# Soft mixture of experts, first half: the down products of one token block as seven half-size products

## The chip, the cores and the metric

One core of a Trainium2 chip runs the whole program in one launch. TensorE (PE) multiplies a 128 x 128 weight tile with up to 512 columns and sums into PSUM, VectorE (DVE), ScalarE (ACT) and GpSimd (POOL) do the elementwise work, and SyncE (SP) issues the DMAs. The metric is the time of one execution on the device in microseconds, the median of several runs.

## What is computed

Three steps follow each other, all in float32 outside and inside: attention with a decay, a gated feed-forward network, and a soft mixture of 8 experts in which every token goes through every expert. The change lies in the last one. There are N = 2304 tokens (4 batches of 576), D = 512, F = 1024 hidden columns for each of E = 8 experts.

```python
def _moe2_ref(x, w_gate, w1, w2):
    P = np.exp(x @ w_gate - max)
    for _ in range(8):                       # balance rows and columns
        P /= P.sum(1, keepdims=True) + 1e-09
        P /= P.sum(0, keepdims=True) + 1e-09
        P *= N / E
    out = np.zeros((N, D))
    for e in range(E):
        h = np.maximum(x @ w1[e], 0.0)       # up product, relu
        ye = h @ w2[e]                       # down product
        out += P[:, e:e + 1] * ye
    return out
```

## The kernel before

**Precision.** Every operand of a product is kept as two tensors, a high part (a copy on ACT, which rounds) and a low part (value minus high part, mostly a subtraction on POOL through the helper `rest`, L163). A product of two such operands is three matmuls (`three`, L171, and the loops in `prod` and `mult`): high with high, high with low, low with high.

**Order of the work.** Attention and the gated network fill the time to about 681 us. Then come 64 slices i = (ph, e, s): two halves `ph` of the tokens (batches 0 and 1, then 2 and 3), in each half 8 experts, and for each expert 4 slices of 256 hidden columns. Slices 0 to 31 are the first half, 32 to 63 the second. A half has two token blocks g of 576 tokens.

**A unit.** For each slice and block `eup(i, g)` (L810) makes one unit. It computes the up product of the block as seven products of half size (`prod`, L827, seven times 6 matmuls of 288 columns into the tile `pa`). Sums of the inputs were made beforehand: those of `x` in `xload` and `xforms`, those of the weights in `wload`, on DVE (`sm` for the first matrix, L749, `sd` for the second, L767). The products are put together by copies `m`, `u` from PSUM (`keep`, L834, ACT), adds `c` (`comb`, L839, DVE) and a relu. Between the seven products a unit runs pieces of down product, handed in as `between` and taken by `fill`.

**Down products in the first half.** `relu` writes the high part `ah` (ACT) and the low part `al` (L849, DVE; from `c`, which lies in SBUF, as `al<-c`, or straight from PSUM as `al<-pa`). The two tiles of `hs[i]` hold all 1152 tokens, in two buffers each. `edown` (L1076) takes tiles of 128 tokens: 6 matmuls of 512 columns into `py` and one DVE add into `acc` (L1098). The second unit of slice i carries tiles 0 to 3 of slice i, the first unit of slice i + 1 carries tiles 4 to 8. A scheduler sets the order of the instructions here, on every engine.

**Down products in the second half.** The relu's result stays in one piece, `rr` (ACT, L844). `form(i, g)` (L890) makes from it the seven left operands: copies on ACT, sums `td` and low parts on POOL (L930 and L163). `fast` (L953) then makes 512 tokens by seven products of half size, in six pieces `s1` to `s6`, here called steps 1 to 6. Step 1 has 12 matmuls of 256 columns, the others 6 each, for two tiles m each, and behind each tile's matmuls stands an add into `acc` (`addto`, L951). Steps 1, 3, 5 and 6 write into the same two PSUM tiles `xy`: step 5 overwrites in place what the adds of step 3 read, step 6 what those of step 5 read. Steps 2 and 4 share the two tiles `zz`. The 64 tokens that are left of each block (`edges`, `eg`) are one tile of `slow`. `queued()` (L885) ties each group of matmuls behind the one before it, so PE's order is the order of the program.

**Weights.** `wload(i)` (L728) loads both matrices of a slice, makes sums, high and low parts, and `wsave(i - 1)` stores all of the slice before to DRAM for the second half, whose `wback` reads them back. The sums `sm`, `sd` (and `td`) share one buffer, so `sm` of one slice waits until the low part `sl` made from `sd` is done. From slice 8 on `xforms` makes and stores the second half's forms of `x` on the side.

**PSUM.** In the first half `ps_z` has 1 bank, `ps_y` (for `py`) 2 and `ps_a` (for `pa`) 5; in the second half `py` and `pa` have 4 each.

## Time and profile before

| | us |
|---|---|
| median of 3 runs | 2187.18 |
| the runs | 2181.81, 2187.18, 2188.16 |
| the profiled execution | 2184.39 |
| its span, first to last instruction | 2182.6 |
| PE busy in the span | 2146.4 (98%) |
| slices 5 to 30, each | 23.54 |
| slices 35 to 62, each | 22.58 |

The time of an execution is the span and 1.8 us around it. Durations in the rows are of the profiled execution. A matmul's own duration in a row is longer than its share of PE, since matmuls overlap: what one costs is read from the starts of those that follow each other. The granted clock of PE is 1.00 of full speed in both halves of the experts.

### The profile page before, as it was taken

The numbers are of one execution on the slowest core, as the hardware profiler recorded it, in microseconds if no ns is written. First come the engines' busy times: TensorE is split into PE (matmuls) and PEld (weight loads), VectorE is DVE, ScalarE is ACT, GpSimd is POOL, SyncE is SP. The second block draws the span as 40 slices with busy tenths as digits, with TensorE's granted clock in tenths as the row PEclk, the third lists the DMA queues.
The fourth block names the chain that finished last, engine by engine and source line by source line (L and its number), as shares of the span: only waits on it lengthen the run. The fifth ranks groups of instructions, "written<-read, shape, count | busy, mean of one in ns | idle before, by whom it ended". The sixth has DMA issues, their size and how long they took to land.

```text
span 2182.6 us, 39368 instructions
## 1 busy us (share of the span) xinstructions
PE 2146.4 (98%) x14941; PEld 1990.3 (91%) x14941; DVE 1382.9 (63%) x2981; ACT 976.5 (45%) x2405; POOL 1121.5 (51%) x1125
## 2 busy tenths in 40 slices
...
GB/s 224 281 234 209 228 173 195 207 159 127 282 175 109 279 191 217 277 202 241 228 238 224 239 225 191 227 377 126 193 170 164 198 146 207 156 178 186 154 209 82
DMA packets 151773, 443.58 MB, mean 203 GB/s; under 512 B 14996, under 2 KB 52224, under 8 KB 139936
## 3 DMA queue, kind: packets, MB, share of 16 engines
...
## 4 chain that ended last, share of the span: by engine, by line
PE 82%; DMA 5%; DVE 4%; ACT 3%; POOL 3%; issue 2%; SPq 0%; POOLq 0%; ACTq 0%; DVEq 0%
PE pa L827 30%; PE py L171 24%; PE py L969 14%; PE pm L171 10%; DMA st<-wf 2%; PE ps_o L444 1%; PE ps_t L416 1%; PE ps_s L320 1%; DMA lgd<-ls 1%; ACT np L295 1%; ACT lead L127 1%; DVE al L849 1%; DVE lead L128 1%; POOL w2l L163 1%; POOL w1l L163 1%
## 5 line engine op out<-in xcount | busy, mean ns | idle before, releaser
L827 PE MATMUL pa<-xf,w1h 128*128 128x288 f32 x3584 | 739.9, 295 | 3.6 <-ACT u L834 2.5
L827 PEld LDWEIGHTS pa<-xf,w1h 128*128 128x128 f32 x3584 | 581.7, 188 | 27.1 <-ACT u L834 3.4
L951 DVE SCALAR_TENSOR_TENSOR acc<-py,lg,acc 128x256 f32<-128x256 f32 (+1 forms) x759 | 386.7, 536 | 219.6 <-PE py L969 189.4
L827 PE MATMUL pa<-xf,w1l 128*128 128x288 f32 x1792 | 523.4, 295 | 0.0
L827 PEld LDWEIGHTS pa<-xf,w1l 128*128 128x128 f32 x1792 | 335.5, 188 | 4.5
L171 PE MATMUL pm<-xh,w 128*128 128x288 f32 x1536 | 327.2, 298 | 1.6 <-ACT xh L459 0.9
L171 PEld LDWEIGHTS pm<-xh,w 128*128 128x128 f32 x1536 | 251.7, 188 | 6.8 <-issue 2.7
L171 PE MATMUL py<-w2h,ah 128*128 128x512 f32 x608 | 239.6, 394 | 4.5 <-DVE acc L1098 4.4
L171 PE MATMUL py<-w2l,ah 128*128 128x512 f32 x608 | 239.2, 393 | 0.0
L171 PE MATMUL py<-w2h,al 128*128 128x512 f32 x608 | 238.5, 393 | 0.0
L1098 DVE SCALAR_TENSOR_TENSOR acc<-py,lg,acc 128x512 f32<-128x512 f32 x252 | 187.2, 746 | 77.9 <-PE py L171 76.6
L171 PE MATMUL pm<-xl,w 128*128 128x288 f32 x768 | 227.3, 296 | 0.7 <-POOL xl L163 0.7
L834 ACT COPY u<-pa 128x288 f32<-128x288 f32 x256 | 101.2, 396 | 212.2 <-PE pa L827 211.8
L163 POOL TENSOR_TENSOR al<-td,ah 128x1024 fp32r<-128x1024 f32 x60 | 144.6, 2410 | 74.6 <-ACT ah L944 74.6
L171 PE MATMUL py<-ah,w 128*128 128x288 f32 x768 | 175.2, 300 | 7.2 <-DVE th L544 3.8
L163 POOL TENSOR_TENSOR al<-th,ah 128x288 fp32r<-128x288 f32 x96 | 79.9, 833 | 194.4 <-ACT ah L545 187.0
L163 POOL TENSOR_TENSOR sl<-sd,sh 128x1024 fp32r<-128x1024 f32 (+1 forms) x40 | 79.6, 1998 | 193.6 <-ACT sh L770 193.5
L849 DVE SCALAR_TENSOR_TENSOR al<-c,ah 128x288 fp32r<-128x288 f32 x192 | 156.3, 829 | 26.5 <-ACT ah L848 23.8
L844 ACT ACTIVATE rr<-c 128x288 f32<-128x288 f32 x192 | 85.4, 445 | 183.5 <-DVE c L839 183.5
L171 PEld LDWEIGHTS pm<-xl,w 128*128 128x128 f32 x768 | 144.5, 188 | 3.0 <-issue 1.4
L839 DVE TENSOR_TENSOR c<-pa,u 128x288 f32<-128x288 f32 x256 | 115.0, 449 | 44.4 <-ACT u L834 32.4
L930 POOL TENSOR_TENSOR td<-rr 128x512 f32<-128x512 f32 x60 | 77.9, 1298 | 126.7 <-ACT eg L905 120.5
...
## 6 DMA issues: line engine op xcount, KB each, us to landing
...
```

What stands on the lines that cost most here:

```text
L127: nc.scalar.activation(out=g, in_=g, func=AF.Relu, scale=8.0, bias=base)
L163: return (eng or nc.gpsimd).tensor_tensor(out=out, in0=src, in1=hi.bitcast(F32), op=ALU.subtract)
L171: ins = nc.tensor.matmul(out=ps, lhsT=a, rhs=b, start=(i == 0), stop=(i == n - 1))
L827: last_pa[0] = nc.tensor.matmul(out=ps, lhsT=w[:, MW[m - 1], k], rhs=x[:, m - 1, hl, k], start=(first and n == 0), stop=(n == len(ops) - 1 ...
L834: nc.scalar.copy(out=t, in_=ps)
L839: last_u[0] = nc.vector.tensor_tensor(out=t, in0=in0, in1=in1, op=ALU.add)
L844: nc.scalar.activation(out=rr[i, g][:, PLACE[f, j]], in_=src, func=AF.Relu)
L849: nc.vector.scalar_tensor_tensor(out=al[:, f, tk], in0=src, scalar=0.0, in1=ah[:, f, tk].bitcast(F32), op0=ALU.max, op1=ALU.subtract)
L930: nc.gpsimd.tensor_tensor(out=t[:, 0:2], in0=b[:, 1:3], in1=b[:, 0:2], op=sub)
L951: nc.vector.scalar_tensor_tensor(out=a, in0=src, scalar=lg[:, TP + t, e:e + 1], in1=a, op0=ALU.mult, op1=ALU.add)
L969: last_pa[0] = nc.tensor.matmul(out=ps, lhsT=x, rhs=y, start=(first and k == 0), stop=(k == 2), skip_group_check=not first)
L1098: nc.vector.scalar_tensor_tensor(out=a, in0=py, scalar=lg[:, t, e:e + 1], in1=a, op0=ALU.mult, op1=ALU.add)
```

## The change

In the first half, block 0 of slices 4 to 30 no longer goes through `edown` but through `form(i, 0)` and `fast(i, 0)`, as the second half does it. Slices 0 to 3 and 31 (the set `direct`) keep the tiles of 512 columns.

- A new function `unit1(i, g)` says what a unit carries. The first unit of slice i carries five tiles of 512 columns of slice i - 1, in the order 5, 4, 6, 7, 8. The second unit of slice i carries steps 1 to 6 of `fast(i - 1, 0)` and, in four pieces, the forms of block 0 of slice i (`front`, `three_`, `middle`, `four`).
- The 64 border tokens of block 0 are put ahead of block 1: `hs[i]` is now 64 + 576 tokens wide, tiles 4 to 8, and has one buffer each instead of two. `rr` of block 0 and the forms `fh`, `fl` have one buffer as well.
- The low part of block 0 is made on POOL (`fl`, from `rr`) and no longer by the four `al` of that block on DVE; those of block 1 stay on DVE.
- `wload2` takes the second matrix out of `wload`: its load, its sums `sd`, its parts and its save come one slice later.
- From slice 4 on PE's order in the first half is tied by `queued()`, in `prod`, `mult` and `edown`.
- The PSUM pools of 4 and 4 banks start at slice 4 instead of 32.
- The gate values of the first half are grouped as those of the second (512 tokens of each block, then the border). Two attention masks move into a pool of their own, freed after the attention.

In numbers of matmuls: 3654 of 256 columns instead of 2520, 1368 `py` of 512 columns instead of 2016. The `al<-c` of DVE go from 192 to 96.

**Order on DVE.** The first list is DVE in the kernel before, around the sums `sm` for the first matrix of slice 17 (`w_12333` is the loaded matrix; `x2` are two in a row).

```order
L849 SCALAR_TENSOR_TENSOR al<-c,ah 128x288 x2
L1098 SCALAR_TENSOR_TENSOR acc<-py,lg,acc 128x512
L767 TENSOR_TENSOR sd<-w_12079 128x256 x2
L1098 SCALAR_TENSOR_TENSOR acc<-py,lg,acc 128x512
L767 TENSOR_TENSOR sd<-sd,w_12079 128x256
L767 TENSOR_TENSOR sd<-w_12079,sd 128x256
L1098 SCALAR_TENSOR_TENSOR acc<-py,lg,acc 128x512
L839 TENSOR_TENSOR c<-pa,u_12289 128x288
L1098 SCALAR_TENSOR_TENSOR acc<-py,lg,acc 128x512
L849 SCALAR_TENSOR_TENSOR al<-c,ah 128x288
L749 TENSOR_TENSOR sm<-w_12333 128x256 x2
L749 TENSOR_TENSOR sm<-sm,w_12333 128x256
```

The second is DVE in the changed kernel in the second unit of slice 15, from the adds of step 1 on.

```order
L1016 SCALAR_TENSOR_TENSOR acc<-py,lg,acc 128x256 x2
L756 TENSOR_TENSOR sm<-w_12810 128x256 x2
L868 TENSOR_TENSOR c<-pa,m_12671 128x288
L756 TENSOR_TENSOR sm<-sm,w_12810 128x256
L1016 SCALAR_TENSOR_TENSOR acc<-py,lg,acc 128x256 x2
L756 TENSOR_TENSOR sm<-w_12810,sm 128x256
L881 SCALAR_TENSOR_TENSOR al<-c,ah 128x288
L1016 SCALAR_TENSOR_TENSOR acc<-py,lg,acc 128x256 x5
L868 TENSOR_TENSOR c<-pa,u_12766 128x288
L1016 SCALAR_TENSOR_TENSOR acc<-py,lg,acc 128x256
L1016 SCALAR_TENSOR_TENSOR acc<-py,lg,acc 128x512
L881 SCALAR_TENSOR_TENSOR al<-c,ah 128x288
```

The sums `sm` stood at the end of a unit, behind the adds; now they stand among the adds of steps 1 and 2, with an `al` behind them, and all of it ahead of the adds of step 3.

**Order on POOL.** Before, the low parts of one slice's weights make up POOL's round, from the `sl` of one slice to that of the next:

```order
L163 TENSOR_TENSOR sl<-sd,sh 128x1024
L163 TENSOR_TENSOR w1l<-w_12333,w1h 128x2x128 x3
L163 TENSOR_TENSOR w1l<-sm,w1h 128x4x2x128
L163 TENSOR_TENSOR w2l<-w_12079,w2h 128x1024
L163 TENSOR_TENSOR sl<-sd,sh 128x1024
```

After, in slice 15 (here `al` of 32 columns are the border tokens' low parts, `rr<-rr` the sums of the forms):

```order
L165 TENSOR_TENSOR al<-rr,ah 128x32
L165 TENSOR_TENSOR sl<-sd,sh 128x1024
L165 TENSOR_TENSOR fl<-rr,fh 128x256
L165 TENSOR_TENSOR al<-rr,ah 128x32 x2
L165 TENSOR_TENSOR fl<-rr,fh 128x512
L165 TENSOR_TENSOR al<-rr,ah 128x32
L999 TENSOR_TENSOR rr<-rr 128x2x256
L1000 TENSOR_TENSOR rr<-rr 128x256
L1001 TENSOR_TENSOR rr<-rr 128x256
L165 TENSOR_TENSOR fl<-rr,fh 128x1024
L165 TENSOR_TENSOR w2l<-w_12812,w2h 128x1024
L165 TENSOR_TENSOR w1l<-w_12810,w1h 128x2x128 x3
```

Between `sl` and the weights' low parts there now stand the low parts and sums of block 0's forms.

The core of the diff:

```diff
@@ -730,6 +731,9 @@
             return
         ph, e, s = slices[i]
         if ph:
+            if i == len(slices) // NPH:
+                wload2(i - 1, True)
+                wload2(i - 1)
             wback(i)
             return
         hold = ExitStack()
@@ -738,9 +742,12 @@
         if i == 1:
             hold.enter_context(tc.issue_after(last_u[0].ins))
         nc.sync.dma_start(out=st, in_=w1[e][:, c0:c0 + FS].rearrange("(k p) f -> p k f", p=P))
-        st2 = wst.tile([P, FS // P, DM], F32, tag="w2", name="w2")
-        last_w[0] = nc.sync.dma_start(out=st2, in_=w2[e][c0:c0 + FS, :].rearrange("(c p) d -> p c d", p=P))
-        wsave(i - 1)
+        if i == 0:
+            wload2(0, True)
+        elif i > 1:
+            wload2(i - 1, True)
+        wsave(i - 1, 0)
+        wsave(i - 2, 1)
         sm = wst.tile([P, 4, 2, P], F32, tag="sm", name="sm", bufs=1)
...
             parts(lo[:, o], src, hi[:, o], 2 if i < EARLY and src is sm else 1)
+        raws[i, 0] = [t.rearrange("p f k c -> p k f c") for t in (hi, lo)]
+        wts[i] = [(hi, lo)]
+        if i != 1:
+            wload2(max(i - 1, 0))
+
+    st2s = {}
+
+    def wload2(i, get=False):
+        ph, e, s = slices[i]
+        c0 = s * FS
+        if get:
+            st2s[i] = wst.tile([P, FS // P, DM], F32, tag="w2", name="w2")
+            last_w[0] = nc.sync.dma_start(out=st2s[i], in_=w2[e][c0:c0 + FS, :].rearrange("(c p) d -> p c d", p=P))
+            return
+        st2 = st2s.pop(i)
+        sub, add = ALU.subtract, ALU.add
+        wsp = (wsp0, wsp1)[i % 2]
...
-        wts[i] = ((hi, lo), (hi2, lo2), (sh, sl))
-        raws[i] = [t.rearrange("p f k c -> p k f c") for t in (hi, lo)] + [hi2, lo2, sh, sl]
+        wts[i] += [(hi2, lo2), (sh, sl)]
+        raws[i, 1] = [hi2, lo2, sh, sl]
 
     wq, raws = {}, {}
 
-    def wsave(i):
+    def wsave(i, part):
         if i < 0:
             return
-        wq[i] = []
-        for n, t in enumerate(raws.pop(i)):
+        wq.setdefault(i, [])
+        for n, t in enumerate(raws.pop((i, part))):
             shape = [P] + [int(x) for x in t.shape[1:]]
-            wq[i].append(dram.tile(shape, F32, name=f"wq{i}_{n}"))
-            nc.sync.dma_start(out=wq[i][n], in_=t.bitcast(F32))
+            wq[i].append(dram.tile(shape, F32, name=f"wq{i}_{2 * part + n}"))
+            nc.sync.dma_start(out=wq[i][-1], in_=t.bitcast(F32))
 
...
@@ -813,8 +838,12 @@
         x = xf[ph * NB + g]
         if ph:
             rr[i, g] = xst.tile([P, 4, HB], F32, tag="x", name="rr", bufs=2)
-        elif g == 0:
-            hs[i] = [hp_.tile([P, 2, NB * S], F32R, tag=t, name=t) for t in ("ah", "al")]
+        elif g:
+            hs[i] = [hp_.tile([P, 2, 64 + S], F32R, tag=t, name=t, bufs=1) for t in ("ah", "al")]
+        elif i in direct:
+            hforms[i, 0] = [formed(t, 4, HB) for t in ("fh", "fl")]
+        else:
+            rr[i, 0] = hp_.tile([P, 4, HB], F32, tag="rr", name="rr", bufs=1)
...
-            with queued() if ph else ExitStack():
+            with queued() if i > EDGES[0] else ExitStack():
...
-            t = hp_.tile([P, HB], F32, tag=tag, name=tag)
+            t = hp_.tile([P, HB], F32, tag="u", name=tag, bufs=4)
...
         def relu(f, j, src):
-            if ph:
+            if (i, g) in rr:
                 nc.scalar.activation(out=rr[i, g][:, PLACE[f, j]], in_=src, func=AF.Relu)
                 return
-            ah, al = hs[i]
-            tk = slice(g * S + j * HB, g * S + (j + 1) * HB)
-            nc.scalar.activation(out=ah[:, f, tk], in_=src, func=AF.Relu)
+            if g:
+                tk = slice(64 + j * HB, 64 + (j + 1) * HB)
+                hi, lo = (t[:, f, tk] for t in hs[i])
+            else:
+                hi, lo = (t[:, PLACE[f, j]] for t in hforms[i, 0])
+            nc.scalar.activation(out=hi, in_=src, func=AF.Relu)
             nc.vector.scalar_tensor_tensor(
-                out=al[:, f, tk], in0=src, scalar=0.0, in1=ah[:, f, tk].bitcast(F32), op0=ALU.max, op1=ALU.subtract)
+                out=lo, in0=src, scalar=0.0, in1=hi.bitcast(F32), op0=ALU.max, op1=ALU.subtract)
 
...
+    last1 = len(slices) // NPH - 1
+    EDGES = (3, last1)
+    direct = {i for i in range(last1 + 1) if i <= EDGES[0] or i == last1}
+
+    def formed(tag, n, w):
+        t = hp_.tile([P, 7 * FS], F32R, tag=tag, name=tag)
+        return t[:, 0:n * w].rearrange("p (n c) -> p n c", n=n)
+
+    def border(i):
+        h, l = hforms[i, 0]
+
+        def ends(n):
+            to, src = hs[i][n][:, :, 0:64], (h, l)[n]
+            for f in range(2):
+                for j in range(2):
+                    o, a = to[:, f, j * 32:(j + 1) * 32], src[:, PLACE[f, j], FS:HB].bitcast(F32)
+                    if n:
+                        nc.gpsimd.tensor_copy(out=o, in_=a)
+                    else:
+                        nc.scalar.copy(out=o, in_=a)
+        return [lambda: ends(0), lambda: ends(1)]
...
+        early = i <= last1
+        if early:
+            edges[i] = [t[:, :, 0:64] for t in hs[i]]
+        elif g == 0:
...
+        def front():
+            nc.scalar.copy(out=h[:, 0], in_=b[:, 0])
+            nc.scalar.copy(out=h[:, 1:3], in_=b[:, 2:4])
+            side(ends_hi)
+
+        def middle():
+            nc.gpsimd.tensor_tensor(out=t[:, 0:2], in0=b[:, 1:3], in1=b[:, 0:2], op=sub)
+            nc.gpsimd.tensor_tensor(out=t[:, 2], in0=b[:, 2], in1=t[:, 0], op=sub)
+            nc.gpsimd.tensor_tensor(out=t[:, 3], in0=b[:, 3], in1=t[:, 2], op=sub)
+
...
-        return [one, two, three_, four]
+        return [front, three_, middle, four] if early else [one, two, three_, four]
 
     def addto(i, a, src, t):
-        e = slices[i][1]
-        nc.vector.scalar_tensor_tensor(out=a, in0=src, scalar=lg[:, TP + t, e:e + 1], in1=a, op0=ALU.mult, op1=ALU.add)
+        ph, e, _ = slices[i]
+        lt = lg[:, ph * TP + t, e:e + 1]
+        nc.vector.scalar_tensor_tensor(out=a, in0=src, scalar=lt, in1=a, op0=ALU.mult, op1=ALU.add)
 
     def fast(i, g):
...
+            if slices[i] == (0, 1, 0):
+                for t in range(4):
+                    nc.scalar.mul(out=acc[:, t], in_=acc[:, t], mul=lg[:, t, 0:1])
...
-            tiles = (range(split, split + 3), range(split + 3, TP))[g]
-            downs = [lambda t=t: edown(d, [t]) for t in tiles]
+            downs = [lambda t=t: edown(d, t) for t in ((5, 4, 6), (7, 8))[g]]
...
+    def unit1(i, g):
+        d = i - 1
+        if g == 0:
+            eup(i, 0, [lambda t=t: edown(d, t) for t in (5, 4, 6, 7, 8)] if i else [])
+            return
+        downs = fast(d, 0) if i and d not in direct else []
+        if i in direct:
+            later = lambda: border(i)
+            downs += [lambda t=t: edown(i, t) for t in range(4)]
+        else:
+            later = lambda: form(i, 0)
+        forms = []
+
+        def begin():
+            forms.extend(later())
+            forms.pop(0)()
+        steps = [begin] + [lambda: forms.pop(0)() if forms else None] * 3
+        downs += [None] * (len(steps) - len(downs))
+        steps += [None] * (len(downs) - len(steps))
+
+        def both(a, b):
+            for f in (a, b):
+                if f:
+                    f()
+        eup(i, 1, [lambda a=a, b=b: both(a, b) for a, b in zip(downs, steps)])
+
+    def edown(i, t):
         ph, e, s = slices[i]
         wb = wts[i][1]
-        ah, al = hs[i]
-        for tt in tiles:
-            t = ph * TP + tt
-            ts_ = slice(tt * P, (tt + 1) * P)
-            py = rooms[0].tile([P, DM], F32, tag="y", name="py")
-            three(py, [((ah[:, c, ts_], al[:, c, ts_]), (wb[0][:, c], wb[1][:, c])) for c in range(2)])
-            a = acc[:, tt, :]
-            if ph == 0 and e == 0:
-
-                if s == 0:
-                    nc.scalar.copy(out=a, in_=py)
-                else:
-                    nc.vector.tensor_tensor(out=a, in0=py, in1=a, op=ALU.add)
+        py = rooms[0].tile([P, DM], F32, tag="y", name="py")
+        if t < 4:
+            j, c = t // 2, slice(t % 2 * P, (t % 2 + 1) * P)
+            left = [[x[:, PLACE[f, j], c] for x in hforms[i, 0]] for f in range(2)]
+        else:
+            c = slice((t - 4) * P, (t - 3) * P)
+            left = [[x[:, f, c] for x in hs[i]] for f in range(2)]
+        with queued() if i > EDGES[0] else ExitStack():
+            ins = three(py, [(left[c], (wb[0][:, c], wb[1][:, c])) for c in range(2)])
+        if i > EDGES[0]:
+            last_pa[0] = ins
...
-        if i == len(slices) // NPH:
+        if i == EDGES[0] + 1:
...
-            tiles = range(split) if g else range(split, TP) if i else ()
-            eup(i, g, [lambda t=t: edown(i if g else i - 1, [t]) for t in tiles])
+            unit1(i, g)
```

## Rows read from the trace of the kernel before

**Rows 1.** The page, busy us, share of the span and instructions of each engine.

```profile
PE 2146.4 (98%) x14941; PEld 1990.3 (91%) x14941; DVE 1382.9 (63%) x2981; ACT 976.5 (45%) x2405; POOL 1121.5 (51%) x1125
```

**Rows 2.** Stages: window, length; busy PE, PEld, DVE, ACT, POOL; clock, DMA, GB/s.

```profile
812.00:1405.00 593.00, 586.04 (x3434) 526.36 (x3433) 446.61 (x784) 240.54 (x531) 265.39 (x181) 1.00 0.62 225
1490.00:2143.00 653.00, 653.00 (x5032) 645.80 (x5031) 425.50 (x898) 300.85 (x811) 458.94 (x581) 1.00 0.46 174
```

**Rows 3.** Timeline, ACT (start, duration): copy of slices 5, 31, 35, 63's first product.

```profile
792.79 0.38 ACT L834 COPY m<-pa 128x288 f32<-128x288 f32 x1
...
1404.96 0.40 ACT L834 COPY m<-pa 128x288 f32<-128x288 f32 x1 [1.05 <-PE pa L827]
...
1511.14 0.40 ACT L834 COPY m<-pa 128x288 f32<-128x288 f32 x1 [0.35 <-PE pa L827]
...
2143.47 0.40 ACT L834 COPY m<-pa 128x288 f32<-128x288 f32 x1 [0.35 <-PE pa L827]
```

**Rows 4.** Timeline of PE, both halves of the experts.

```profile
1036.23 0.39 PE L171 MATMUL py<-w2h,ah 128*128 128x512 f32 x1
...
1037.38 0.39 PE L171 MATMUL py<-w2h,al 128*128 128x512 f32 x1
...
1526.76 0.28 PE L969 MATMUL py<-sh,ah 128*128 128x256 f32 x1
...
1527.47 0.43 PE L827 MATMUL pa<-xf,w1h 128*128 128x288 f32 x2
...
1527.87 0.42 PE L827 MATMUL pa<-xf,w1h 128*128 128x288 f32 x2
```

**Rows 5.** Timelines of POOL and DVE around 1366 us.

```profile
1366.08 2.50 POOL L163 TENSOR_TENSOR w1l<-w,w1h 128x256 fp32r<-128x256 f32 x3
...
1366.15 1.82 DVE L749 TENSOR_TENSOR sm<-w 128x256 f32<-128x256 f32 x2 [1.39 <-POOL sl L163]
1367.90 0.96 DVE L749 TENSOR_TENSOR sm<-sm,w 128x256 f32<-128x256 f32 x1
```

**Rows 6.** Timelines of POOL, DVE and PE, 1033 to 1040 us.

```profile
1035.58 2.62 POOL L163 TENSOR_TENSOR w2l<-w,w2h 128x1024 fp32r<-128x1024 f32 x1
...
1033.35 5.17 DVE L849 SCALAR_TENSOR_TENSOR al<-c,ah 128x288 fp32r<-128x288 f32 x2
...
1038.44 0.74 DVE L1098 SCALAR_TENSOR_TENSOR acc<-py,lg,acc 128x512 f32<-128x512 f32 x1
...
1039.23 0.50 PE L171 MATMUL py<-w2h,ah 128*128 128x512 f32 x1 [0.92 <-DVE acc L1098]
```

**Rows 7.** DVE groups, 812 to 1405 us: busy us, mean ns, idle before, releaser.

```profile
L849 DVE SCALAR_TENSOR_TENSOR al<-c,ah 128x288 fp32r<-128x288 f32 x152 | 125.3, 841 | 23.0 <-ACT ah L848 20.7
...
L749 DVE TENSOR_TENSOR sm<-w 128x256 f32<-128x256 f32 x48 | 28.0, 618 | 9.1 <-POOL sl L163 8.3 <-DMA wq<-sh 0.8
...
L767 DVE TENSOR_TENSOR sd<-w 128x256 f32<-128x256 f32 x48 | 18.3, 420 | 26.5 <-DMA w<-w 26.4
```

**Rows 8.** Waits of PE, 812 to 1405 us: total us, times, longest.

```profile
PE py L171 <- DVE acc L1098: 4.2, 6, 1.5
```

**Rows 9.** Timeline of DVE in the second half.

```profile
1527.32 0.88 DVE L951 SCALAR_TENSOR_TENSOR acc<-py,lg,acc 128x256 f32<-128x256 f32 x2 [0.61 <-PE py L969]
1528.81 0.48 DVE L951 SCALAR_TENSOR_TENSOR acc<-py,lg,acc 128x256 f32<-128x256 f32 x1 [0.62 <-PE py L969]
```

**Rows 10.** POOL groups, 1490 to 2143 us: busy us, mean ns, idle before.

```profile
L163 POOL TENSOR_TENSOR al<-td,ah 128x1024 fp32r<-128x1024 f32 x58 | 139.8, 2411 | 72.0 <-ACT ah L944 72.0
...
L930 POOL TENSOR_TENSOR td<-rr 128x512 f32<-128x512 f32 x58 | 75.3, 1298 | 120.5 <-ACT eg L905 120.5
L163 POOL TENSOR_TENSOR al<-rr,ah 128x512 fp32r<-128x512 f32 x58 | 75.1, 1294 | 0.0
L163 POOL TENSOR_TENSOR eg<-rr,eg 128x32 fp32r<-128x32 f32 x232 | 56.3, 253 | 1.5 <-ACT eg L905 0.4
L163 POOL TENSOR_TENSOR al<-rr,ah 128x256 fp32r<-128x256 f32 x58 | 42.7, 736 | 0.0
```

82 lines of the change are left out of this document (48 added, 34 removed).

## The prediction

> **What bounds the kernel now.** I read the page first: TensorE (PE) is busy 98% of the span [rows 1], so only two things can move the time: fewer or shorter matmuls, and places where PE waits. The table by stage then shows the two halves of the experts side by side [rows 2]: the first (812 to 1405 us) and the second (1490 to 2143 us). In the second half both token blocks already use the seven half-size products, so it is the model for what the first half is to become; but its POOL is busy 70% and its VectorE (DVE) 65%, while the first half has POOL at 45% and DVE at 75%. From the copies of each slice's first product I take the slice lengths [rows 3]: slices 5 to 30 take (1404.96 - 792.79)/26 = 23.54 us each, slices 35 to 62 take (2143.47 - 1511.14)/28 = 22.58 us. The order of PE gives what a slice holds: 84 up products of 288 columns and 54 down products of 512 before; in the second half 84 of 288, 84 of 256 and 6 of 512.
>
> Starts that follow each other give the price of one [rows 4]: 512 columns (1037.38 - 1036.23)/5 = 0.230 us, 256 columns (1527.47 - 1526.76)/6 = 0.118 us, 288 columns (1527.87 - 1527.47)/3 = 0.133 us. The first half's 84 x 0.133 + 54 x 0.230 = 23.6 us is its whole slice: it runs dense today. Its waits for DVE are small, 4.2 us in 593 us [rows 8].
>
> **What the change removes.** In 27 slices (4 to 30) the four tiles of the first block take 42 products of 256 columns instead of 24 of 512: 24 x 0.230 - 42 x 0.118 = 0.56 us less. The second half's slice, taken whole, gives (22.58 - 84 x 0.133 - 6 x 0.230)/84 = 0.119 us for the 256-column one, and so 0.52 us. I take 0.53 us, 27 times: -14 us.
>
> Here the Trainium skill speaks against the change: TensorE: Matmul & The Clock Gate, section Back-to-back issue gap, gives for sustained pairs of weight load and matmul 81 ns at 128 columns and 131 ns at 512. Between them 256 columns would be 98 ns (an estimate from that page), and 42 x 98 ns against 24 x 131 ns a loss of 1.0 us a slice, +26 us. The rows say 118 and 230, nearly halved, so the measurement decides and this gets no chance.
>
> **What it adds.** (1) ScalarE (ACT) gets some 3 us of copies a slice; it was busy 41% of this stage [rows 2] and stays far from full. Nothing waits on it that did not before. (2) POOL gets the low parts and sums of one block. In the second half two blocks cost 458.94/653 x 22.58 = 15.9 us a slice, one 7.9; with the 265.39/593 x 23.54 = 10.5 it has now, 18.4 of 23 us, 79%. As a sum that fits. (3) DVE loses the four low parts of that block and gets ten adds of 256 and two of 512 columns for four of 512; by count about +1 us, 65 to 80% busy. (4) Second-matrix forms a slice later: their loads and saves on SP move with them; the products that use them move a slice later too, so the cover (a whole slice of PE work) stays. If it were gone, the first 512-column product of a slice would wait for the low part. 0. (5) Slices 0 to 4 and the change to the second half (31, 32): the four downs missing from slice 4 come back as slice 31's; the reload of the x forms keeps 16 us of PE work in front of it. 0, within 4 us either way.
>
> **The term that decides: who holds DVE.** Where a DVE instruction reads two SBUF tensors (`sm`, `sd`, `al<-c`) while POOL runs one of its own, it ends only 0.3 us after POOL's instruction has ended. It shows [rows 5] in three POOL pieces back to back from 1366.08 to 1368.58 with two `sm` beside them in 1.82 us and a third in 0.96 us, one per POOL piece, in turns; `sd`, which finds POOL idle, takes 0.42 [rows 7]. `al<-c` averages 841 ns for the same reason [rows 7]. Adds into `acc` (one input in PSUM) are not held: 0.48 us each, 0.40 apart, with POOL at 70% [rows 2, 9]. The whole chain is there in the kernel of today [rows 6]: an `al` held until 1038.5 by a POOL piece that ends at 1038.20, the add behind it done at 1039.18, PE idle 0.92 us until 1039.23. The Trainium skill has a rule for it (SBUF — State Buffer, section Who interferes with whom: a DVE instruction with two SBUF inputs contends with a GpSimd instruction that reads SBUF, and whichever issues first blocks the other). By it half of the held instructions would be those that came first and waited for nothing, and the sum below would halve, to rival (b); [rows 5] show each `sm` behind a piece of its own, so the measurement decides.
>
> Today this costs PE little, since the first half's order leaves the `sm` for moments when POOL is idle and its hidden values are double buffered. The new order has neither. In 15 of the 27 slices (8, 12, 14 to 17, 21, 23 to 30) DVE stands as in the order shown: two adds, `sm` twice, `c`, `sm`, two adds, `sm`, `al`, then the adds of steps 3, 4, 5. `sm` can't start before POOL's `sl` is done, and right behind that `sl` POOL runs 0.74, 0.25 twice, 1.29, 0.25, 1.30, 0.74, 0.74 = 5.56 us without a gap (durations of the same pieces [rows 10]; the two 256-column sums taken like the 736 ns row).
>
> Now the second unit, from the start of step 1 (a product of 6 x 0.133 = 0.80, a step of 6 x 0.118 = 0.71). PE: step 1 to 1.42, product to 2.22, step 2 to 2.93, product, step 3 to 4.44, product, step 4 to 5.95, product to 6.75, step 5 to 7.46, product to 8.26, step 6 to 8.97, product to 9.77. An add starts 0.20 after its matmuls' slot (1526.76 + 3 x 0.118 = 1527.12, add at 1527.32) [rows 4, 9]. DVE unhindered: adds at 0.91 and 1.62 to 2.02; `sm` twice (0.34 each, 420 ns less the 0.08 overlap of rows 9) 2.70; `c` (0.38, estimated as 288/256 of that) 3.08; `sm` 3.42; adds 4.22; `sm` 4.56; `al` 4.94; first add of step 3 at 4.94. Step 5 overwrites what that add reads; it needs its end (0.48) and 0.05 [rows 6], so a start by 6.22. Slack: 1.28 us. The five held instructions each find POOL in a piece; the mean rest of one is the sum of squares over twice the sum, 5.18/11.1 = 0.47 us, together 2.3 us. Bounds: nothing, if POOL lies elsewhere, and the five longest pieces, 4.8 us; I take 2.3, since [rows 5] show one piece per instruction.
>
> So step 5 starts 1.0 us late (7.77). DVE still owes the other add of step 3, two of step 4, then step 5's (8.84, 9.62 with a `c` between); step 6's second half waits until 10.15 and the unit ends at 11.31, not 9.77: 1.5 us. Behind it the next unit's first 512-column product needs the last `al<-pa`, which stands behind two 512-column adds and an `al` that POOL can hold: 0 to 0.6, I take 0.2. So 1.7 us in these 15 slices. The other 12 have the `sm` elsewhere (ahead of step 1, or behind step 3): 0.3 to 1.7, I take 1.0. Sum 15 x 1.7 + 12 x 1.0 = +37 us. Most of today's 4.2 us of waits goes: -4.
>
> **Sum.** -14 + 37 - 4 = +19 us. The profiled execution took 2184.4 us, span 2182.6 and 1.8 around it; the median is 2187.2. 2187 + 19 = **2206 us**, slices of 24.3 us.
>
> **Rivals.** (a) PE stays dense: POOL's pieces fall beside the adds, as PE in the second half never waits for them. For it: the second half, with POOL busier than DVE. Against: there DVE has no two-SBUF instruction at all. -14 - 4 + 4 (0.15 a slice) = 2173 us. (b) Half the waits: 0.65 us a slice, 18 us, cancels: 2187 us. The point between (a) and mine is the slack: up to 1.28 us of held time in a unit costs step 5 nothing. (c) Held at the long pieces, 2.8 us a slice on the mean: 76 - 18 = +58, 2245 us; for it, POOL's 1024-column piece (2.41 us) standing across the last `al`; against, that POOL's order puts it past step 5. (d) The change not doing what it says: its order on PE has 1134 more 256-column products and 648 fewer of 512, so no.
>
> **Chances.** Forecast 0.53 (2195 to 2222), (a) 0.22, (b) 0.14, (c) 0.11. The range goes from (a) with all of today's waits gone, 2187 - 14 - 4 = 2169, to 2234; it leaves out a fifth of (a) and most of (c), some 0.15. This kernel can be told from no change at about 0.3% (6.6 us). Faster: (a) and a little of (b), 0.25; same: 0.14; slower: 0.61.
>
> **What would show it.** Slices 5 to 30 some 24.3 us long (22.9 under (a)); PE waiting for DVE `acc`, at the half-size products, 25 to 45 us in that stage; `sm` above 0.75 us on the mean (0.62 now) and `sd` still 0.42; POOL 70 to 80% busy. I would be wrong if `sm` stayed at 0.6, if the chain had DMA (the later second matrix) in PE's waits, or if slices before 5 or around 31 moved by more than 4 us.

## The result, and the profile after

The changed kernel takes 2214.85 us (median of 4 runs, 2212.88 to 2217.94) against 2185.8 for the kernel before (4 runs): a ratio of 1.0136, 95% interval [1.0115, 1.0157]. It is 29 us slower. The forecast was 2206, the range 2169 to 2234. The profiled execution is one of 2217.94 us, with a span of 2216.2, 33.6 us more than the 2182.6 of before.

The page after, busy us and share of the span of each engine, then the stage that answers to the first of [rows 2], with its columns: window, length, busy PE, PEld, DVE, ACT, POOL, clock, DMA share, GB/s.

```profile
PE 2157.6 (97%) x15427; PEld 2016.9 (91%) x15427; DVE 1422.1 (64%) x3089; ACT 1041.5 (47%) x2614; POOL 1355.9 (61%) x1415
...
828.00:1424.00 596.00, 572.41 (x3741) 529.22 (x3741) 467.32 (x856) 285.51 (x675) 462.70 (x417) 0.99 0.60 219
```

In the first half of the experts POOL has gone from 45% to 78%, DVE from 75% to 78%, and PE, dense before, now has 24 us in which nothing runs on it. The slices, by the copy of their first product as in [rows 3] (slices 5, 24, 25 and 31):

```profile
803.74 0.38 ACT L863 COPY m<-pa 128x288 f32<-128x288 f32 x1
...
1277.33 0.39 ACT L863 COPY m<-pa 128x288 f32<-128x288 f32 x1
...
1301.78 0.39 ACT L863 COPY m<-pa 128x288 f32<-128x288 f32 x1
...
1447.65 0.38 ACT L863 COPY m<-pa 128x288 f32<-128x288 f32 x1
```

Slices 5 to 30 take (1447.65 - 803.74)/26 = 24.77 us each (23.54 before, 24.3 forecast). Slice 24 takes 24.45, and so do those behind it up to 29.

**A ledger.** To see where 33.6 us come from I count the matmuls between two slice starts and price them by what their starts stand apart in a dense stretch (medians: 0.2315 us for 512 columns, 0.1332 for 288, 0.1188 for 256). What is left of the stage is time in which PE did not run at that rate.

| slices | work before | left before | work after | left after |
|---|---|---|---|---|
| 0 to 4 | 107.1 | 4.5 | 108.7 | 13.9 |
| 5 to 30 | 605.5 | 6.7 | 601.0 | 42.9 |
| 31 to 33 | 82.5 | 1.1 | 70.2 | 3.5 |
| 34 to 62 | 654.0 | 0.9 | 654.0 | 1.4 |
| sum | 1449.2 | 13.2 | 1433.9 | 61.7 |

The work has shrunk by 15.3 us, as the counts of matmuls say; 48.5 us of waiting have come in, 36 of them in slices 5 to 30. (In the kernel before, part of the downs lagged behind into slices 31 to 33; the work per stage shifts by that.)

**One steady unit.** The second unit of slice 27, in the timelines of PE, POOL and DVE (start, duration):

```profile
1366.05 0.28 PE L1034 MATMUL py<-sh,fl 128*128 128x256 f32 x1
...
1368.33 0.29 PE L856 MATMUL pa<-xf,w1l 128*128 128x288 f32 x1
1369.36 0.39 PE L1034 MATMUL py<-sh,fh 128*128 128x256 f32 x1 [0.74 <-DVE acc L1016]
...
1371.68 0.39 PE L1034 MATMUL py<-w2h,fh 128*128 128x256 f32 x1
```

```profile
1360.94 2.40 POOL L165 TENSOR_TENSOR sl<-sd,sh 128x1024 fp32r<-128x1024 f32 x1 [1.03 <-ACT sh L794]
1363.30 0.74 POOL L165 TENSOR_TENSOR fl<-rr,fh 128x256 fp32r<-128x256 f32 x1
1363.99 0.84 POOL L165 TENSOR_TENSOR al<-rr,ah 128x32 fp32r<-128x32 f32 x2
1364.79 1.29 POOL L165 TENSOR_TENSOR fl<-rr,fh 128x512 fp32r<-128x512 f32 x1
1366.04 0.44 POOL L165 TENSOR_TENSOR al<-rr,ah 128x32 fp32r<-128x32 f32 x1
1366.43 1.28 POOL L999 TENSOR_TENSOR rr<-rr 128x512 f32<-128x512 f32 x1
1367.80 0.80 POOL L1000 TENSOR_TENSOR rr<-rr 128x256 f32<-128x256 f32 x1
1368.67 0.82 POOL L1001 TENSOR_TENSOR rr<-rr 128x256 f32<-128x256 f32 x1
```

```profile
1363.76 0.95 DVE L756 TENSOR_TENSOR sm<-w 128x256 f32<-128x256 f32 x2
...
1365.01 1.35 DVE L756 TENSOR_TENSOR sm<-sm,w 128x256 f32<-128x256 f32 x1
1366.29 0.86 DVE L1016 SCALAR_TENSOR_TENSOR acc<-py,lg,acc 128x256 f32<-128x256 f32 x2
1367.07 0.93 DVE L756 TENSOR_TENSOR sm<-w,sm 128x256 f32<-128x256 f32 x1
1367.92 0.99 DVE L881 SCALAR_TENSOR_TENSOR al<-c,ah 128x288 fp32r<-128x288 f32 x1
1368.84 2.04 DVE L1016 SCALAR_TENSOR_TENSOR acc<-py,lg,acc 128x256 f32<-128x256 f32 x5
```

Behind `sl` POOL runs from 1363.30 to 1369.5 almost without a gap. The `sm` that starts at 1365.01 ends at 1366.36, 0.28 us after the 1.29 us piece of POOL (1366.08); the next `sm` ends at 1368.00, 0.29 after the piece that ends at 1367.71; `al` at 1368.91, 0.31 after 1368.60. So the adds of step 3, whose last matmul started at 1366.05, begin only at 1368.84, and step 5, due at 1368.46 on PE, starts at 1369.36: 0.90 us late. Step 6 then starts its second tile 0.30 late (1371.68). Together 1.2 us, and 0.2 in smaller pieces.

### The profile page after: what moved, and what is told of

The parts are those of the page before. It is cut to its first block, busy times and chain, and to the rows that moved or that the text cites. A ratio compares the mean times of both kernels' runs of the same rounds, so it can differ in the third digit from the quotient of the medians.

```text
span 2216.2 us, 41043 instructions
## 1 busy us (share of the span) xinstructions
PE 2157.6 (97%) x15427; PEld 2016.9 (91%) x15427; DVE 1422.1 (64%) x3089; ACT 1041.5 (47%) x2614; POOL 1355.9 (61%) x1415
## 4 chain that ended last, share of the span: by engine, by line
PE 71%; DVE 9%; POOL 7%; DMA 6%; ACT 4%; issue 4%; SPq 0%; POOLq 0%; ACTq 0%; DVEq 0%
PE pa L856 24%; PE py L173 16%; PE py L1034 16%; PE pm L173 11%; DVE sm L756 2%; POOL w1l L165 2%; DVE acc L1016 2%; DMA st<-wf 1%; PE ps_o L445 1%; POOL fl L165 1%; PE ps_t L417 1%; POOL sl L165 1%; ACT np L296 1%; PE ps_s L321 1%; DMA lgd<-ls 1%
## 5 line engine op out<-in xcount | busy, mean ns | idle before, releaser
L1016 DVE SCALAR_TENSOR_TENSOR acc<-py,lg,acc 128x256 f32<-128x256 f32 (+1 forms) x1227 | 652.5, 556 | 333.2 <-PE py L1034 218.4
L165 POOL TENSOR_TENSOR fl<-rr,fh 128x512 fp32r<-128x512 f32 (+3 forms) x205 | 256.6, 1252 | 53.2 <-ACT fh L1008 39.8
L1034 PE MATMUL py<-sh,fh 128*128 128x256 f32 x696 | 200.0, 287 | 18.4 <-DVE acc L1016 18.2
L873 ACT ACTIVATE rr<-c 128x288 f32<-128x288 f32 x273 | 121.4, 445 | 202.7 <-DVE c L868 199.2
L1034 PE MATMUL py<-sh,fl 128*128 128x256 f32 x696 | 196.2, 282 | 0.0
L1034 PE MATMUL py<-sl,fh 128*128 128x256 f32 x696 | 196.0, 282 | 0.0
L165 POOL TENSOR_TENSOR fl<-td,fh 128x1024 fp32r<-128x1024 f32 x60 | 144.4, 2407 | 75.2 <-ACT fh L1008 75.2
L1034 PE MATMUL py<-w2h,fh 128*128 128x256 f32 x522 | 151.8, 291 | 2.8 <-DVE acc L1016 1.1
L1034 PEld LDWEIGHTS py<-sh,fh 128*128 128x128 f32 x696 | 132.2, 190 | 24.3 <-DVE acc L1016 24.1
L1034 PE MATMUL py<-w2h,fl 128*128 128x256 f32 x522 | 147.0, 282 | 0.0
```

Source lines behind the costliest of these rows:

```text
L165: return (eng or nc.gpsimd).tensor_tensor(out=out, in0=src, in1=hi.bitcast(F32), op=ALU.subtract)
L873: nc.scalar.activation(out=rr[i, g][:, PLACE[f, j]], in_=src, func=AF.Relu)
L1016: nc.vector.scalar_tensor_tensor(out=a, in0=src, scalar=lt, in1=a, op0=ALU.mult, op1=ALU.add)
L1034: last_pa[0] = nc.tensor.matmul(out=ps, lhsT=x, rhs=y, start=(first and k == 0), stop=(k == 2), skip_group_check=not first)
```

## The experiments

Each kernel was timed beside the kernel before, and its ratio is to that. The "left" columns are those of the ledger.

| kernel | median us | ratio | 95% interval | left 0-4 | 5-30 | 31-33 |
|---|---|---|---|---|---|---|
| after | 2214.85 | 1.0136 | 1.0115 to 1.0157 | 13.9 | 42.9 | 3.5 |
| e2_no_lows | 2179.84 | 0.9981 | 0.9971 to 0.9991 | 13.8 | 7.9 | 8.0 |
| e1_direct_all | 2227.16 | 1.0201 | 1.0186 to 1.0216 | 12.3 | 37.6 | 8.0 |
| e9_direct_spread | 2210.53 | 1.0123 | 1.0102 to 1.0144 | 16.2 | 26.8 | 3.2 |
| e15_direct_free | 2190.4 | 1.0031 | 1.0021 to 1.0042 | 7.2 | 6.8 | 5.4 |
| e4_xt_pool | 2218.39 | 1.0161 | 1.0146 to 1.0176 | 13.5 | 45.6 | 3.9 |
| e5_scale | 2217.18 | 1.0146 | 1.0127 to 1.0166 | 15.6 | 42.2 | 5.0 |
| e12_sm_late | 2234.44 | 1.0232 | 1.0216 to 1.0248 | 12.7 | 60.9 | 6.0 |
| e13_sm_xt_late | 2234.93 | 1.0234 | 1.0218 to 1.0249 | 12.7 | 60.7 | 6.5 |
| e6_sm_pool | 2199.26 | 1.0075 | 1.0056 to 1.0095 | 11.6 | 26.9 | 4.0 |
| e17_sm_c | 2189.81 | 1.0021 | 1.0009 to 1.0032 | 12.7 | 15.2 | 6.4 |
| e18_sm_c_xt | 2203.22 | 1.0089 | 1.0073 to 1.0105 | 13.4 | 31.6 | 4.6 |
| e19_all | 2188.84 | 1.0020 | 1.0010 to 1.0031 | 16.5 | 9.1 | 4.5 |

### Is it POOL that makes DVE late?

```diff
-        h, l = hforms[i, g] = [formed(t, 7, FS) for t in ("fh", "fl")]
+        h, l = hforms[i, g] = [formed("fh", 7, FS)] * 2 if early else [formed(t, 7, FS) for t in ("fh", "fl")]
...
         def middle():
-            nc.gpsimd.tensor_tensor(out=t[:, 0:2], in0=b[:, 1:3], in1=b[:, 0:2], op=sub)
...
+            pass
...
-            rest(l[:, 3:7], t, h[:, 3:7])
+            early or rest(l[:, 3:7], t, h[:, 3:7])
```

> The changed kernel, but POOL's work on block 0's forms of the first half is left out: the three subtractions in `middle` and the low parts `fl` (some 7 us a slice); the matmuls read the high part in their place, so the result lacks these low parts and sums. The same matmuls, adds and DVE instructions run. Theory (POOL's pieces hold DVE): `sm` falls below 0.55 us on the mean, the wait ahead of step 5 (0.9 us in slices 24 to 30) goes, the slices take 23.0 to 23.3 us, the time falls by 25 to 36 us to 2180 to 2190 us. Rival (DVE has too many adds, sums and low parts in that stretch, POOL or not): the wait ahead of step 5 stays at 0.5 us or more, the time above 2203 us.

Groups by form of DVE, 828 to 1424 us (busy us, mean ns of one, idle time before); first after, then this kernel:

```profile
L881 DVE SCALAR_TENSOR_TENSOR al<-c,ah 128x288 fp32r<-128x288 f32 x72 | 63.6, 883 | 2.9 <-ACT ah L880 2.3
...
L756 DVE TENSOR_TENSOR sm<-w 128x256 f32<-128x256 f32 x48 | 28.1, 623 | 2.2 <-POOL sl L165 2.1
L756 DVE TENSOR_TENSOR sm<-sm,w 128x256 f32<-128x256 f32 x24 | 27.4, 1143 | 0.0
...
L756 DVE TENSOR_TENSOR sm<-w,sm 128x256 f32<-128x256 f32 x24 | 21.0, 876 | 0.0
```

```profile
L881 DVE SCALAR_TENSOR_TENSOR al<-c,ah 128x288 fp32r<-128x288 f32 x75 | 38.1, 508 | 2.5 <-ACT ah L880 0.5
...
L756 DVE TENSOR_TENSOR sm<-sm,w 128x256 f32<-128x256 f32 x24 | 11.6, 484 | 0.0
...
L756 DVE TENSOR_TENSOR sm<-w,sm 128x256 f32<-128x256 f32 x24 | 10.0, 418 | 0.0
```

The same DVE instructions without those pieces beside them: 508 and not 883 ns for `al<-c`, less than half for the two `sm`. The waits of PE for the adds, in the same stretch (total us, times, longest), after and here:

```profile
PE py L1034 <- DVE acc L1016: 18.6, 23, 2.4
```

```profile
PE py L1034 <- DVE acc L1016: 1.0, 4, 0.3
```

Slices 24 to 29 take 23.07 us, the time falls by 35 us to 2179.84, at the low edge of what the theory gave. The adds are as many as before; it is POOL's pieces that make them late. DVE's order is not quite the same, since with POOL free the first two `sm` of a unit come ahead of the adds of step 1; but the held time alone is enough: from start to start the four `sm` and the `al` of a steady unit take 3.92 us after and 1.89 us here, so 2.0 us are held time, and without these the adds of step 3 in slice 27 would begin at 1366.8, in time for step 5. With 2179.84 this is also what rival (a) would have looked like: 3 us below the kernel before, and not 14, since what is left in slices 0 to 4 and 31 to 33 stays.

### How much is the fixed order?

```diff
-    direct = {i for i in range(last1 + 1) if i <= EDGES[0] or i == last1}
+    direct = set(range(last1 + 1))
```

> The change without its seven half-size products: all slices of the first half keep the tiles of 512 columns for block 0 (no `rr`, no forms on POOL). Everything else of the change stays: TensorE's fixed order, hidden values in one buffer, second matrix a slice later, 4 + 4 PSUM banks from slice 4. Theory (DVE's instructions with two SBUF inputs are held by POOL's pieces of the forms): without those pieces the steady slices are as long as before, 23.5 to 23.8 us, and the time is 2183 to 2196 us, with what slice 4 and the change to the second half cost. Rival (the fixed order and the single buffers stall TensorE, not the forms): the slices stay above 24.2 us, the time at 2205 or more.

2227.16, slower even than the change: the theory missed, and slices and time lie on the rival's side. In its steady slices PE waits 0.65 us for the copy `u`, always in the same place: with the four tiles of a second unit spread as the changed kernel spreads them, nothing is left to stand between two products that share a bank. That is a fault of this experiment, so it was made again with the tiles where the kernel before has them.

```diff
-        spare = len(rest_) > 3
+        spare = len(rest_) > 4
```

> As e1_direct_all (no half-size down products in the first half), but the four tiles of a second unit stand where the kernel before has them, so that one of them lies between the second product and the third and one ahead of the fourth: in e1_direct_all PE waited 0.65 us in every slice for the copy `u` with nothing in between. Theory (fixed order, single buffers and later second matrix cost little by themselves): steady slices 23.5 to 23.8 us, 2190 to 2205 us, what is left are the slices with `xt` (7, 11, 16, 20) and slice 4. Rival (the fixed order and the single buffers cost as much as the forms): slices at 24.2 or more, 2215 or more.

2210.53, between the two expectations: neither theory had it. Half of the steady slices take 23.59 us, the other half 24.45. The timelines of POOL, DVE and PE show what is left:

```profile
1386.58 2.66 POOL L165 TENSOR_TENSOR w2l<-w,w2h 128x1024 fp32r<-128x1024 f32 x1 [0.87 <-ACT w2h L786]
```

```profile
1386.54 0.45 DVE L881 SCALAR_TENSOR_TENSOR fl<-c,fh 128x288 fp32r<-128x288 f32 x1
1386.91 2.61 DVE L756 TENSOR_TENSOR sm<-w,sm 128x256 f32<-128x256 f32 x1
...
1389.81 0.44 DVE L881 SCALAR_TENSOR_TENSOR fl<-pa,fh 128x288 fp32r<-128x288 f32 x1
```

```profile
1390.31 0.50 PE L173 MATMUL py<-w2h,fl 128*128 128x512 f32 x1 [0.58 <-DVE fl L881]
```

It is the same mechanism with another holder: an `sm` of 0.4 us takes 2.61 beside the low part of the second matrix, the low part `fl<-pa` behind it comes late, and PE, whose order is fixed, waits for it. (The `fl<-c` that starts at 1386.54, just ahead of POOL's piece, is not held.) The next experiment gives the order back to the scheduler and leaves the buffers single.

```diff
-            with queued() if i > EDGES[0] else ExitStack():
+            with queued() if ph else ExitStack():
...
-        with queued() if i > EDGES[0] else ExitStack():
+        with queued() if i > last1 else ExitStack():
```

> As e9_direct_spread (512 columns throughout, hidden values in one buffer, second matrix a slice later, 4 + 4 banks), but PE's order in the first half left to the scheduler as in the kernel before. e9_direct_spread is 26 us slower than before, most of it PE waiting 0.8 to 3.8 us for a low part `fl` that POOL holds. Theory A (the fixed order leaves PE nothing to do beside such a wait): 2183 to 2194 us. Theory B (the single buffers make PE wait, whatever the order): 2204 us or more.

2190.4: 20 us of e9_direct_spread's 26 are gone, and theory A holds. POOL holds DVE no less here (DVE's group by form, 828 to 1400 us):

```profile
L881 DVE SCALAR_TENSOR_TENSOR fl<-c,fh 128x288 fp32r<-128x288 f32 x72 | 90.4, 1255 | 7.5 <-ACT fh L880 5.3
```

1255 ns for a `fl` that takes some 0.45 us free, and that took 627 ns in e9_direct_spread (the scheduler moved DVE's and POOL's instructions too). But PE has other matmuls to run in the meantime. So the single buffers, the bank split and the later second matrix together cost some 6 us (ratio 1.0031), and the fixed order is what turns a held DVE instruction into a wait of PE.

### The four slices that are longer still

Slices 7, 11, 16 and 20 of the changed kernel take 26.8 to 27.5 us, their neighbours 24.5. DVE and PE in slice 7:

```profile
866.39 2.38 DVE L689 TENSOR_TENSOR xt<-xst 128x288 f32<-128x288 f32 x2
```

```profile
867.53 0.29 PE L856 MATMUL pa<-xf,w1l 128*128 128x288 f32 x1
869.22 0.39 PE L1034 MATMUL py<-sh,fh 128*128 128x256 f32 x1 [1.39 <-DVE acc L1016]
```

The sums `xt` of the second half's x stand among the adds as well, are held as `sm` is, and PE loses 1.55 us in one wait. Behind it, the stage 871.20 to 874.50 (columns as above):

```profile
871.20:874.50 3.30, 3.30 (x17) 3.23 (x16) 2.80 (x8) 1.37 (x3) 1.40 (x1) 0.50 0.01 2
```

The granted clock is 0.50, the lower of the two levels, and the starts of the matmuls stand 0.24 us apart at 288 columns and not 0.133: some 1.5 us lost. There are five such stretches among the experts of the changed kernel (behind waits of 1.5 to 3.3 us), 7.5 us in all, and none in the kernel before.

```diff
-                nc.vector.tensor_tensor(out=o, in0=x, in1=y, op=ALU.subtract)
+                nc.gpsimd.tensor_tensor(out=o, in0=x, in1=y, op=ALU.subtract)
```

> The changed kernel with the four sums of x for the second half (`xt` in `xforms`, 4 parts of 4 sums) on POOL and not on DVE; the result is the same. Theory (these DVE instructions with two SBUF inputs are held as well, and make slices 7, 11, 16 and 20 some 2.5 us longer than their neighbours, about half of it waiting and 1.4 us of it a clock that falls to 1.2 GHz behind a wait above 2 us): those four slices come to 24.2 to 24.8 us, the time falls by 8 to 12 us to 2203 to 2208. Rival (in these slices the DMA or POOL's low parts of x hold TensorE): under 3 us.

2218.39: nothing gained. Slices 7, 11, 16 and 20 do come down (25.2 to 25.9 us), and no wait of 2 us nor a stretch at the lower clock is left in them. But the slices behind them take 26.8, 26.8, 27.0 and 25.7 us (24.8, 25.9, 24.6 and 25.5 in the changed kernel), and three of them (8, 12 and 17) now have the wait and the stretch: the granted clock is 0.50 for some 3.3 us from 876.3, 978.7 and 1105.0 us. (The "wait above 2 us" of the expectation isn't right for slice 7 of the changed kernel, where it is 1.55.) Two lines of PE's waits, 828 to 1424 us:

```profile
PE py L1034 <- DVE acc L1016: 12.2, 20, 0.8
PE py L173 <- DVE al L881: 9.1, 9, 2.0
```

The wait for the adds has shrunk and one for the low part `al` has come in its place: POOL's longer row of pieces holds `al` (`al<-c` 1011 ns on the mean in this stretch, 883 after). A held instruction taken off DVE and given to POOL came back here as more time in which the others are held.

### Slice 4

ACT and PE around 795 us, where the changed kernel has its longest wait:

```profile
795.53 1.33 ACT L1191 ACTIVATE acc<-acc,lg 128x512 f32<-128x512 f32 x2
...
797.57 1.03 ACT L786 CAST w2h<-w 128x1024 fp32r<-128x1024 f32 x1
798.50 0.39 ACT L863 COPY u<-pa 128x288 f32<-128x288 f32 x1
```

```profile
798.94 0.53 PE L856 MATMUL pa<-xf,w1h 128*128 128x288 f32 x2 [3.10 <-ACT u L863]
```

```diff
         def s1():
-            if slices[i] == (0, 1, 0):
-                for t in range(4):
-                    nc.scalar.mul(out=acc[:, t], in_=acc[:, t], mul=lg[:, t, 0:1])
             for m in range(2):
+                scale(1, m)
...
             for m in range(2):
+                scale(0, m)
```

> The changed kernel, where the four scalings of `acc` on ACT, all ahead of step 1 of slice 4's seven products, stand one by one ahead of the first add of their tile. Theory (the four in a row wait for slice 3's adds and hold the copy `u` behind them, 3.1 us in which TensorE waits, and the clock falls behind it): 2 to 5 us less, 2209 to 2213. Rival (slice 4 waits for the new forms themselves): under 2 us.

2217.18: no gain. I had moved the wrong scalings: the ones that stand ahead of `u` are at L1191, in `edown`, those of tiles 4 to 8, and with them stand the other copies of the rows above. What else would shorten slice 4 was not settled (see e19_all).

### Moving the sums

```diff
+            with tc.issue_after(last_lo[0].ins) if i > 5 else ExitStack():
-            nc.vector.tensor_tensor(out=sm[:, o], in0=x, in1=y, op=op)
+                nc.vector.tensor_tensor(out=sm[:, o], in0=x, in1=y, op=op)
```

Here `last_lo` is the last low part `al` of a second unit.

> The changed kernel, the same work, but DVE's four sums `sm` of each slice from 6 on come behind the last low part `al` of a second unit, so at the start of the next first unit, and no more among the adds of steps 1 and 2. Theory (the held `sm` are what makes step 3's adds late): the wait ahead of step 5 goes from 0.9 us to 0 to 0.2 us; the held time moves to the first unit, where five tiles of 512 columns give more room; steady slices 23.0 to 23.5 us, 2185 to 2195 us in all, since slices 7, 11, 16, 20 (sums `xt`) and slice 4 stay long. Rival (the adds of step 3 are late in any case, by the number of adds in that unit): slices stay above 24 us, the time above 2205.

2234.44, 20 us worse than the change: by the numbers (slices of 25.2 us) the rival's side, but not for the rival's reason. The `sm` are out of the way and step 5 of most units starts in time; but POOL's row of pieces has moved too. POOL, DVE and PE, 1354 to 1359 us:

```profile
1354.99 2.42 POOL L165 TENSOR_TENSOR fl<-rr,fh 128x1024 fp32r<-128x1024 f32 x1 [1.16 <-ACT fh L1009]
```

```profile
1355.29 2.44 DVE L882 SCALAR_TENSOR_TENSOR al<-c,ah 128x288 fp32r<-128x288 f32 x1 [0.39 <-ACT ah L881]
...
1358.31 0.44 DVE L882 SCALAR_TENSOR_TENSOR al<-pa,ah 128x288 fp32r<-128x288 f32 x1
```

```profile
1358.80 0.50 PE L173 MATMUL py<-w2h,al 128*128 128x512 f32 x1 [0.49 <-DVE al L882]
```

An `al` now falls beside the 1024-column piece and ends 0.32 us after it (1357.73 and 1357.41), an `al<-pa` waits behind it, and with it the first 512-column product of the next unit, which reads that low part. In the first unit the held `sm` make a `c` late as well: 14.6 us of PE's waits are for `c`.

The next one adds the same tie to the sums `xt` (the edit is the last one of e19_all, below).

> As e12_sm_late, and the sums `xt` for the second half's x behind a second unit's last `al` too. Theory: slices 7, 11, 16, 20 come down to 23.0 to 24.5 us as well, some 6 to 10 us below e12_sm_late, 2176 to 2188 us. Rival (these slices are long by x's low parts on POOL or by its DMAs, wherever the sums stand): within 3 us of e12_sm_late.

2234.93, the same as e12_sm_late, as the rival had it: with `al` and `c` late in every slice, the place of the `xt` decides nothing here. That it can decide something e19_all shows.

Then, instead of another time, another engine:

```diff
-            nc.vector.tensor_tensor(out=sm[:, o], in0=x, in1=y, op=op)
+            (nc.gpsimd if i > 5 else nc.vector).tensor_tensor(out=sm[:, o], in0=x, in1=y, op=op)
```

> The changed kernel with the four sums `sm` of each slice from 6 on on POOL and not on DVE; the same result. Theory (a sum on POOL can't be held by POOL): the wait ahead of step 5 falls below 0.3 us, POOL goes to 88 to 92% busy; 2185 to 2200 us. Rival (POOL then becomes what bounds): PE waits for POOL's low parts `w1l`, `w2l`, `fl`, slices above 24.2 us, 2205 or more.

2199.26, within the theory's range, with POOL at 518 of 572 us, 91%. But `al<-c` is held longer than in the changed kernel (883 ns), and waits for it have come in (828 to 1400 us):

```profile
L881 DVE SCALAR_TENSOR_TENSOR al<-c,ah 128x288 fp32r<-128x288 f32 x71 | 90.2, 1271 | 7.4 <-ACT ah L880 5.3
```

```profile
PE py L173 <- DVE al L881: 8.7, 10, 2.0
```

### Taking the second input out of SBUF

```diff
-            t = hp_.tile([P, HB], F32, tag="c", name="c")
+            t = hp_.tile([P, HB], F32, tag="c", name="c") if to is None or not g or ph or i <= EDGES[0] else to()
...
-        relu(0, 0, comb(prod(2, bank()), m1))
+        p2 = prod(2, bank())
+        relu(0, 0, comb(p2, m1, lambda: p2))
...
-        relu(1, 1, comb(pz, u3))
+        relu(1, 1, comb(pz, u3, bank))
```

This is made on e6_sm_pool; the third `c` of a unit is written to `pz` in the same way.

> As e6_sm_pool (sums `sm` on POOL), and the adds `c` of block 1 write to PSUM, not to SBUF, so that `al<-c` reads one SBUF tensor and one in PSUM; the same result. Theory (two SBUF inputs are what gets held): `al<-c` falls from 0.9 to 1.0 us to 0.45 us, the waits of PE for `al` and `acc` (together 17 us in e6_sm_pool) fall to 8 us or less, those of the slices with `xt`; 2184 to 2193 us. Rival (the PSUM banks, held longer by these adds, make PE wait for `pa`): 2197 or more.

The group of low parts and PE's waits, 828 to 1400 us (by name all four are `al<-pa` now; three of them read the result of `c`):

```profile
L881 DVE SCALAR_TENSOR_TENSOR al<-pa,ah 128x288 fp32r<-128x288 f32 x96 | 42.7, 450 | 5.7 <-ACT ah L880 3.6
```

```profile
PE py L1035 <- DVE acc L1017: 8.2, 10, 1.5
```

2189.81, as expected. With POOL at 90% of the stage, the 96 low parts take 450 ns on the mean, none more than 0.46 us; the wait for `al` is gone, and slices 25 to 29 take 23.07 us, as in e2_no_lows, with all of POOL's work done. This is the plainest answer of the study: what is held is an instruction with two inputs in SBUF, and one input in PSUM frees it. The sums `sd`, whose inputs are still both in SBUF, stay held in the same stretch: 588 to 683 ns on the mean of their three groups. PE's waits for the adds, 8.2 us, lie nearly all in the slices with `xt`.

With the edit of e4_xt_pool on top:

> As e17_sm_c, and the sums `xt` on POOL. Theory: with no DVE instruction but `sd` left that POOL can hold, slices 7, 11, 16 and 20 come to 23 to 24.5 us; 2174 to 2184 us, below the kernel before. Rival (POOL, above 90% busy in those slices, is late with the weights' low parts): no better than e17_sm_c.

2203.22, 13 us worse: by the time the rival's side. The rival's reason is not what the trace shows, though: PE waits for no low part of the weights, but above all for the adds (828 to 1400 us):

```profile
PE py L1035 <- DVE acc L1017: 13.7, 14, 3.3
```

The `sd` stand among these adds and are held longer, 722 to 870 ns on the mean: ahead of the longest of the waits two of them take 4.61 us. So here too it is POOL that holds DVE.

The last kernel is e17_sm_c with both scalings (of tiles 0 to 3 and, in `edown`, of 4 to 8) on DVE, and `xt` behind `last_lo`:

```diff
-                    nc.scalar.mul(out=acc[:, t], in_=acc[:, t], mul=lg[:, t, 0:1])
+                    nc.vector.tensor_scalar_mul(out=acc[:, t], in0=acc[:, t], scalar1=lg[:, t, 0:1])
...
+                with tc.issue_after(last_lo[0].ins):
-                nc.vector.tensor_tensor(out=o, in0=x, in1=y, op=ALU.subtract)
+                    nc.vector.tensor_tensor(out=o, in0=x, in1=y, op=ALU.subtract)
```

> As e17_sm_c, with the sums `xt` behind a second unit's last `al` (so in the first unit, where e17_sm_c shows no wait) and the scalings of `acc` in slice 4 on DVE and not on ACT. Theory: slices 7, 11, 16 and 20, 24.9 to 26.7 us in e17_sm_c, come to 23 to 24.5 us (6 to 10 us in all), and slice 4's wait of 2.0 us for the copy behind the scalings goes; 2175 to 2184 us, the kernel before or a little below. Rival (held sums `xt` in the first unit delay its adds of 512 columns, as the `sm` did in e12_sm_late): 2187 us or more.

2188.84, by the time the rival's side, but for another reason. Slices 7, 11, 16 and 20 take 22.9 to 24.5 us, as the theory said, and slices 5 to 30 have 9.1 us left, against 6.7 in the kernel before, while all slices together have 15 us less work. What spoils it are slices 0 to 4: 16.5 us left against 4.5. The scalings on DVE made PE's waits there longer, not shorter. The gain of the half-size products does arrive where they stand, and is lost ahead of and behind them. No kernel of this study beats the kernel before by more than the 0.3% that a measurement can tell; e2_no_lows, which leaves work out, comes nearest.

## Why the prediction was right, and where it was not

**The bound, and what the change removes.** Right. PE was dense, and the work of the matmuls, at the ledger's prices, shrank by 15.3 us (forecast 14) [rows 3, 4]. Whole slices give less. The 23.54 us of before are a mean over slices that hold 52 down products on the mean and some of them waits; those with just 84 up and 54 down products and no wait (16 and 17) take 23.49. In e2_no_lows a slice takes 23.07: 0.42 us saved, forecast 0.53, and so 11 us in 27 slices.

**The term that decides.** Right in mechanism, in place and nearly in size. The order foretold where the `sm` would stand and which row of POOL's pieces would lie beside them; the trace shows both, each held instruction ending 0.28 to 0.31 us after a piece of POOL as in [rows 5]. The mean of the four `sm` is (48 x 623 + 24 x 1143 + 24 x 876)/96 = 816 ns (forecast above 0.75 us). The 0.62 us of [rows 7] was no mean of the four, though, but that of the first group, which stands at 623 ns after; over all four the kernel before has 546 ns. Two of the signs were not met: `sd` was to stay at 0.42 us and took 0.49, and PE's waits for `acc` come to 18.6 us in the view, where 25 to 45 were forecast (the view counts the time in which PE stands still, 0.74 us where step 5 of slice 27 is 0.90 late). The sum for slices 4 to 30 was +37 - 4 = +33; what is left in slices 5 to 30 grew by 36.2.

Inside that sum two sizes were off, to opposite sides, so that it came so near is in part luck: by the ledger the 15 slices that the prediction names have 19.4 us left (forecast 25.5), the other eleven of 5 to 30 have 23.5 (forecast 11). A steady unit lost 1.4 us and not 1.7: step 5 was 0.90 late (forecast 1.0), step 6 0.30 (forecast 0.5), and the last `al<-pa` cost next to nothing (forecast 0.2). The four slices with `xt`, on the other side, lost some 4 us each: the prediction never counted the sums `xt` among the instructions with two SBUF inputs, though they are four per part and stand beside the adds. Nor did it count what PE's clock takes behind a long wait: 6.0 us in these slices.

**Slices 0 to 4 and the change to the second half.** Here a term was mis-sized. The prediction put it at 0, within 4 us; slices 0 to 4 measured +9.4 (waits of PE: 3.6 us for the copy `u`, the longest 3.1 with ACT's scalings and forms ahead of it, 1.7 for an add and 0.8 for the copy `m`; and 1.5 us of lower clock) and slices 31 to 33 +2.4, in which stands a wait for a DMA, the reload of the second half's weights (1424 to 1530 us; the kernel before has none there):

```profile
PE pa L856 <- DMA w1l<-wq: 1.9, 1, 1.9
```

Together that is more than the 9 us between 2206 and 2214.85. The prediction had named both as signs of being wrong (more than 4 us before slice 5; a DMA in PE's waits, though there it thought of the second matrix), and for this term they came true.

**ACT, the later second matrix, the buffers.** Costed at nothing; e15_direct_free bears it out within 6 us, as a sum. That the fixed order is a cost of its own the prediction did not say ("The new order has neither" speaks of where the `sm` stand and of the buffers): e9_direct_spread and e15_direct_free put 20 us on it for the 512-column tiles. With the half-size products and a free order nothing was tried, so how much of the change's 29 us a free order would give back stays open.

**The rivals.** (a), a dense PE, is what e2_no_lows shows once POOL's pieces are gone: the point from which it decides, held time in the unit, was right. (b) and (c) were the same mechanism at other sizes, and the measured one lies between the forecast and (c). The loss that the prediction estimated from the figures of the Trainium skill (TensorE: Matmul & The Clock Gate, section Back-to-back issue gap: 81 ns at 128 columns and 131 ns at 512) did not show: starts stand 0.119 us apart at 256 columns and 0.232 at 512, and e2_no_lows gains 0.42 us per slice.

The Trainium skill, SBUF — State Buffer, section Who interferes with whom, says that two SBUF inputs on DVE contend with a GpSimd instruction that reads SBUF, and whichever issues first blocks the other. The trace agrees on who is held (e17_sm_c: 450 ns with one input in PSUM, against 1271 in e6_sm_pool with both in SBUF). It agrees on who comes first as well: in e9_direct_spread the `fl<-c` of 1386.54, ahead of POOL's piece by 0.04 us, takes its free 0.45 us, and that piece takes 2.66 us where one of 1024 columns takes 2.41 [rows 10]. So page and rows agree here, where the prediction took them to differ; what failed was its step from the rule to half the sum. Of the 280 DVE instructions with two SBUF inputs between 828 and 1424 us of the changed kernel, 191 began inside a piece of POOL, 87 met none and only 2 began ahead of one: POOL's pieces are the longer ones and often stand without a gap, so where the two meet POOL is nearly always first.
